# Adding batch 0's band mask on TensorE instead of multiplying it on VectorE, with k's rows in natural order

## The chip, the cores and the metric

The kernel runs on one core of one Trainium2 chip. Times are device microseconds (us) of a whole execution. The median of three executions of the kernel before was 313.24 us (312.52 to 313.91); with the fourth that ran beside the changed kernel, 313.38, it is 313.31. Executions of one kernel agree to some tenths of a per cent. "PE" is TensorE, "PEld" its weight load, "DVE" VectorE, "ACT" ScalarE, "POOL" GpSimd, "SP" SyncE. A profile has a span 1.7 to 2.0 us shorter than the time of the execution that it was taken from.

## The reference

```python
# q_l, k_l, v_l: (8, 8, 512, 64); q_g, k_g, v_g: (8, 8, 32, 64); all f32
mask = np.abs(pos[:, None] - pos[None, :]) <= 32      # band, for local x local
s_ll = np.where(mask, scale * q_l @ k_l.T, -1e9)
s_lg = scale * q_l @ k_g.T
out_l = softmax([s_lg, s_ll]) @ [v_g; v_l]            # local queries
out_g = softmax(scale * q_g @ [k_g; k_l].T) @ [v_g; v_l]
x = concat([out_g, out_l]) -> (8 * 544, 512)          # heads side by side
h = x @ w_in                                          # 512 -> 2048
g = h * sigmoid(1.702 * h)
out = g @ w_out                                       # 2048 -> 512, f32
```

Attention over a band of 32 positions to either side and 32 global positions is followed by a two-layer MLP. The MLP's matmuls are most of the work.

## The kernel before

The eight heads of a batch are two units ("quads") of four heads; `a` is unit 0 and `c` is unit 1 of batch 0. For a quad, `Tk` and `Tq` transpose k and q on DVE, `S(rnd)` makes half of the scores on PE (key blocks 0 and 1, or 2 and 3, each against a window of queries), `X` takes the exp on ACT, `M` multiplies by the 0/1 band mask on DVE, `K` and `XK` do the global keys, `U` and `ekU` multiply by v. Row position is split as 16 r + t for queries and, before, in 4 r + t for keys.

```python
kf = k_l.rearrange("b (u j) (c r t) d -> b j r u c (t d)", j=4, c=4, t=4)
vf = v_l.rearrange("b h (c r t) d -> b t r h c d", c=4, t=4)
...
load(0, kq=False)
q32 = ld.tile([128, 16 * D], F32, name="q32", bufs=1)
nc.scalar.dma_start(out=q32, in_=qf[0][:, 0])        # q of unit 0, f32, ScalarE's queue
load_g32(0, "qk")                                     # globals, SyncE's queue
load_g32(0, "v", eng=nc.scalar)
for j in range(4):
    load_k(0, 0, j)                                   # k of unit 0, to bf16, POOL's queue
...
keep(62, psP.tile([128, 512], F32, name="w", tag="p"), 128)   # warm-up matmuls
...
def Tk(self, cs=(0, 1, 2, 3)):
    ...
    nc.vector.transpose(self.kT[:, cs], rk[:, cs])    # keys stay in the order (t r)

def S(self, rnd, split=False, warm=0):
    ...
    for c in (2 * rnd, 2 * rnd + 1):
        for e in range(2):
            for j in range(4):
                nc.tensor.matmul(ps[j][:, off : off + n * nr],
                                 lhsT=self.k[p, 128 * c : 128 * c + 128, e],
                                 rhs=self.q[p, t0 : t0 + n, r0 : r0 + nr, e],
                                 start=(e == 0), stop=(e == 1), skip_group_check=True)

def M(self, rnd, lo=0, hi=LW):
    e = self.E[rnd][:, :, at + lo : at + hi]
    nc.vector.tensor_mul(e, e, mask[:, rnd : rnd + 1, lo:hi].to_broadcast(...))
...
# batch 0, in program order (cut)
make_mb(); cast_q(0); cast_q(1); make_mask()          # masks built ahead of all else
... a.S(0); a.X(0); a.S(1, split=True, warm=4); a.X(1)
... a.M(0); c.Tq(); c.gg(); c.S(0); c.X(0); a.M(1)
load_g32(1, "qkv", hold=True)
... c.S(1); c.X(1, halves=True) ... c.M(0) ... c.M(1, 0, 192); c.M(1, 192)
... # then the first four h steps of the MLP, fc = 0 to 3, and fc = 4 to 15
```

The softmax here doesn't subtract the row's maximum and nothing guards it: scores larger than these inputs give would overflow.

## Time and profile before

| | before |
|---|---|
| median time | 313.24 us |
| span of the profile | 310.7 us |
| PE busy | 97% |
| first S of unit 0 / of unit 1 | 7.90 / 11.81 us |
| first h matmul of the MLP | 20.19 us |
| first matmul of the second MLP layer | 34.41 us |
| first S of batch 2 | 66.01 us |

The stages in this table are start times from the span's start, read from the timeline of PE. Two lines of the page of the kernel before will be needed later; the prediction shows the rest. The first is the granted PE clock in 40 slices of the span, the second a group of instructions (shapes, count, busy us and mean ns, idle time before).

```profile
PEclk9999999999999999999999999999999999999999
...
L260 DVE STREAM_TRANSPOSE kT<-rk 128x512 f32<-128x512 f32 (+1 forms) x17 | 11.4, 671 | 0.0
```

### The profile page before, as it was taken

Reading aid. Unit: us, or ns where it says so; the run is one execution under the profiler, and the core shown is the slowest. Engines: PE = TensorE matmul, PEld = TensorE weight load, DVE = VectorE, ACT = ScalarE, POOL = GpSimd, SP = SyncE. Lnnn points to the kernel's source line nnn. Section 1 sums busy time; section 2 is a strip of 40 time slices with the busy share of each in tenths; the row PEclk is TensorE's granted clock in tenths of the full one; section 3 lists DMA queues with packets and bytes.
Section 4 is the critical chain, followed back from the end, with each engine's and each line's share of the span. In section 5 each row is a group of like instructions: output and inputs, shape, how many; then the busy total and the mean of one; then the engine's idle time right before and its main releaser. Section 6 shows DMA issues by size and latency. Waiting matters only on the chain.

```text
span 310.7 us, 7885 instructions
## 1 busy us (share of the span) xinstructions
PE 302.8 (97%) x3257; PEld 148.6 (48%) x3257; DVE 210.4 (68%) x463; ACT 167.3 (54%) x254; POOL 80.0 (26%) x131
## 2 busy tenths in 40 slices
PE   7899999999999999999999999999999999999995
PEld 6444444444554454444454455444454454446653
DVE  7887946869867866776957866776767855574320
ACT  4817465476536744565446735565556652563321
POOL 8822579677146000900045001200000000000000
PEclk9999999999999999999999999999999999999999
DMA  8999999999969212970279113901120012201123
GB/s 154 149 189 207 206 161 193 165 147 129 151 77 168 45 36 61 139 108 12 60 77 169 30 36 71 102 0 31 41 49 23 0 38 55 48 0 29 41 61 76
DMA packets 60099, 27.44 MB, mean 88 GB/s; under 512 B 43296, under 2 KB 51744, under 8 KB 60064
## 3 DMA queue, kind: packets, MB, share of 16 engines
q0 software_dynamic: 51536, 17.11, 50.7%
q1 hardware_dynamic: 7904, 9.12, 11.9%
q10 hardware_dynamic: 624, 0.72, 0.8%
q8 instruction: 25, 0.41, 0.5%
q14 instruction: 10, 0.08, 0.1%
HBM read 35.13 MB, written 8.91 MB: 142 GB/s over the span
## 4 chain that ended last, share of the span: by engine, by line
PE 91%; DVE 3%; ACT 2%; DMA 1%; POOL 1%; issue 0%; ACTq 0%; DVEq 0%; POOLq 0%
PE op L482 37%; PE hp L457 36%; PE s L291 6%; PE ov L389 5%; PE ov L367 3%; DMA rk<-in_k_l_dram 1%; PE s L457 1%; ACT e L322 1%; PE kb L310 1%; DVE e L329 1%; PE op L494 1%; PE s L310 1%; DVE gT L465 1%; PE s L406 1%; POOL rk L84 1%; PE ov L162 1%
## 5 line engine op out<-in xcount | busy, mean ns | idle before, releaser
L482 PE MATMUL op<-w_out_sb,gT 128*128 128x512 bf16 x528 | 121.9, 380 | 0.1
L465 DVE SCALAR_TENSOR_TENSOR gT<-th,hp 128x512 bf16<-128x512 f32 (+1 forms) x140 | 91.1, 655 | 43.0 <-ACT th L464 42.4
L457 PE MATMUL hp<-xL,w_in_sb 128*128 128x512 bf16 x496 | 108.6, 379 | 0.3 <-DVE xL L421 0.3
L464 ACT ACTIVATE th<-hp 128x512 f32<-128x512 f32 (+1 forms) x140 | 79.9, 573 | 43.7 <-PE hp L457 41.2
L457 PEld LDWEIGHTS <-w_in_sb 128*128 128x128 bf16 x576 | 56.1, 98 | 65.1 <-issue 1.2
L482 PEld LDWEIGHTS <-gT 128*128 128x128 bf16 x528 | 49.3, 98 | 56.2 <-issue 3.3
L322 ACT ACTIVATE e<-s 128x1712 bf16<-128x1712 f32 (+2 forms) x32 | 49.6, 1552 | 15.8 <-PE s L406 8.9
L496 ACT ACTIVATE ob<-op 128x512 f32<-128x512 f32 (+2 forms) x35 | 20.5, 585 | 61.6 <-PE op L482 59.1
L97 POOL DMA_DIRECT2D v<-in_v_l_dram x36 | 27.0, 757 | 96.2 <-PE s L406 88.9
L84 POOL DMA_DIRECT2D rk<-in_k_l_dram x64 | 34.9, 557 | 12.3 <-DMA w_in_sb<-in_moe_w_in_dram 4.7
L329 DVE TENSOR_TENSOR e<-e,mask 128x1408 bf16<-128x1408 bf16 (+2 forms) x33 | 28.0, 851 | 6.9 <-ACT e L322 6.7
L412 DVE STREAM_TRANSPOSE sT<-ov 128x512 f32<-128x512 f32 x16 | 11.4, 714 | 31.3 <-PE ov L389 31.3
L291 PE MATMUL s<-q,kT 32*128 32x200 bf16 (+1 forms) x512 | 21.3, 284 | 1.5 <-DVE kT L260 0.9
L421 DVE TENSOR_TENSOR xL<-ov,rs 128x512 bf16<-128x512 f32 x32 | 20.7, 685 | 2.2 <-PE ov L389 0.9
L291 PEld LDWEIGHTS <-kT 32*128 32x128 bf16 x512 | 10.9, 95 | 14.7 <-issue 9.1
L357 ACT ACTIVATE ek<-kb 128x512 bf16<-128x512 f32 x16 | 9.6, 600 | 8.4 <-PE kb L310 8.4
L389 PE MATMUL ov<-e,v 128*32 128x192 bf16 (+1 forms) x512 | 13.1, 240 | 0.0
L416 DVE STREAM_TRANSPOSE rs<-rT 128x512 f32<-128x512 f32 x16 | 11.4, 711 | 0.6
L260 DVE STREAM_TRANSPOSE kT<-rk 128x512 f32<-128x512 f32 (+1 forms) x17 | 11.4, 671 | 0.0
L263 DVE STREAM_TRANSPOSE q<-rq 128x512 f32<-128x512 f32 (+1 forms) x17 | 10.9, 647 | 0.0
L389 PEld LDWEIGHTS <-v 128*32 128x32 bf16 x512 | 9.8, 97 | 2.0 <-issue 2.0
L310 PE MATMUL kb<-q,kgT 32*32 32x512 bf16 x128 | 10.0, 385 | 0.5 <-ACT e L319 0.5
(71 smaller groups left out, 155.5 us busy)
## 6 DMA issues: line engine op xcount, KB each, us to landing
out_dram<-ob SPq DMA_DIRECT2D x132, 64.0 KB, 1.7
rk<-in_k_l_dram POOLq DMA_DIRECT2D x64, 64.0 KB, 4.0
v<-in_v_l_dram POOLq DMA_DIRECT2D x28, 128.0 KB, 4.5
rq<-in_q_l_dram POOLq DMA_DIRECT2D x6, 512.0 KB, 6.7
w_in_sb<-in_moe_w_in_dram POOLq DMA_DIRECT2D x4, 512.0 KB, 11.7
w_out_sb<-in_moe_w_out_dram POOLq DMA_DIRECT2D x4, 512.0 KB, 13.4
rq<-in_q_l_dram POOLq DMA_DIRECT2D x3, 256.0 KB, 7.9
q<-in_q_l_dram ACTq DMA_DIRECT2D x1, 512.0 KB, 3.9
```

The costliest lines, as they stand in the source:

```text
L84: nc.gpsimd.dma_start(out=loaded[b][0][32 * j : 32 * j + 32, u], in_=kf[b, j][:, u])
L97: nc.gpsimd.dma_start(out=vtiles[b % 2][p, s, :, :, :D], in_=vf[b, t][:, hs])
L291: nc.tensor.matmul(ps[j][:, off : off + n * nr], lhsT=self.k[p, 128 * c : 128 * c + 128, e], rhs=self.q[p, t0 : t0 + n, r0 : r0 + nr, e], ...
L322: nc.scalar.activation(e[:, :, lo:hi], self.ps[:, :, lo:hi], AF.Exp, scale=scale)
L329: nc.vector.tensor_mul(e, e, mask[:, rnd : rnd + 1, lo:hi].to_broadcast([128, 4, hi - lo]))
L389: nc.tensor.matmul(ov[32 * j : 32 * j + 32, :].rearrange("p (t r) -> p t r", t=16)[:, :, r0 : r0 + nr], lhsT=lv, rhs=self.E[c // 2][:, j, ...
L421: nc.vector.tensor_mul(self.x[:, 2 * self.u + h, :], self.st[1 + h], self.st["rs"])
L457: nc.tensor.matmul(hp[:, : width(i)], lhsT=w_in_c[:, fc // 8, kc, fc % 8 // 2, :, fc % 2], rhs=(xL[i] if i < B else xG)[:, kc, :], start=( ...
L464: nc.scalar.activation(th[:, :n], hp[:, :n], AF.Tanh, scale=0.851)
L465: nc.vector.scalar_tensor_tensor(gTs[i][:, fc, :n], in0=th[:, :n], scalar=1.0, in1=hp[:, :n], op0=ALU.add, op1=ALU.mult)
L482: nc.tensor.matmul(op, lhsT=gTs[i][:, fc, tci * 128 : tci * 128 + 128], rhs=w_out_sb[:, fc, :], start=(first and fc == 4 * f4), stop=(fc = ...
L496: nc.scalar.activation(ob[:, lo:hi], op[:, lo:hi], AF.Copy, scale=0.5)
```

## The change

The intent: take four mask multiplies and the building of the mask off the ladder of engines that leads to the first h matmul. In batch 0 the band is added to the scores as a large negative bias, by an identity matmul that opens each PSUM accumulation (`B`). For that the keys have to lie in natural order, so that one band serves all blocks; k is therefore written in that order by its transpose (and v is read in that order). The 0/1 mask that later batches need is built by ACT among batch 0's h steps. In passing, half of k of unit 0 is loaded as f32 from SyncE, v of unit 0 comes ahead of that of unit 1, and the first half of w_in comes in narrower pieces.

```diff
-    vf = v_l.rearrange("b h (c r t) d -> b t r h c d", c=4, t=4)
+    vf = v_l.rearrange("b h (c t r) d -> b t r h c d", c=4, t=4)
...
+    k32 = ld.tile([128, 2, 4 * D], F32, name="k32", bufs=1)
+    load_g32(0, "q")
     for j in range(4):
-        load_k(0, 0, j)
+        nc.sync.dma_start(out=k32[32 * j : 32 * j + 32], in_=kf[0, j][:, 0, 0:2])
+    load_g32(0, "kv")
...
-    keep(62, psP.tile([128, 512], F32, name="w", tag="p"), 128)
+    keep(44, psP.tile([128, 512], F32, name="w", tag="p"), 128)
...
+    nc.vector.tensor_sub(ident, step[:, 65:193], step[:, 64:192])
+    nc.vector.tensor_sub(band, step[:, 65:257], step[:, 0:192])
+    nc.vector.tensor_scalar(bias, band, -1.0, 240000.0, op0=ALU.add, op1=ALU.mult)
+
+    def window(t, c):
+        y0 = 0 if c else 32
+        return t[:, y0 : y0 + 16 * WIN[c][1]].rearrange("p (r t) -> p t r", t=16)
...
-            nc.vector.transpose(self.kT[:, cs], rk[:, cs])
+            nc.vector.transpose(self.kT[:, cs].rearrange("p (c r t) -> p c t r", r=32, t=4), rk[:, cs])
...
+        def B(self, rnd, split=False, cs=(0, 1)):
+            ...
+                for j in range(4):
+                    nc.tensor.matmul(ps[j][:, w : w + 16 * WIN[c][1]], lhsT=ident, rhs=window(bias, c),
+                                     start=(c == 2 * rnd), stop=False, skip_group_check=True)
...
-    a.S(0)
+    a.B(0)
+    a.B(1, split=True)
+    a.S(0, added=True)
...                      # likewise c.B(0), and c.B(1) in two halves; a.M, c.M of batch 0 gone
-    load_g32(1, "qkv", hold=True)    # moved to after a.R()
...
     for fc in range(4, FC):
         h_step(0, fc)
+        if fc in (5, 6, 8, 9):
+            make_mask((5, 6, 8, 9).index(fc))
```

`window(bias, c)` reads the bias with its inner index 16 elements apart, that is every 32 bytes in bf16. The output of the transpose of k goes to every fourth f32, that is every 16 bytes.

More of the change, by code (lines that the diff above doesn't have):

```diff
@@ L135 @@
     q32 = ld.tile([128, 16 * D], F32, name="q32", bufs=1)
-    nc.scalar.dma_start(out=q32, in_=qf[0][:, 0])
-    load_g32(0, "qk")
-    load_g32(0, "v", eng=nc.scalar)
-    for j in range(4):
-        load_k(0, 0, j)
-    mk = consts.tile([32, 208], BF16)
-    nc.vector.memset(mk, 1.0)
-    for sg, base in ((1, 2 * W + 3), (-1, -3)):
-        nc.gpsimd.affine_select(
-            out=mk, in_=mk, pattern=[[-sg, 208]], compare_op=ALU.is_ge,
-            fill=0.0, base=base, channel_multiplier=4 * sg,
-        )
+    for hf in range(2):
+        f = slice(8 * D * hf, 8 * D * hf + 8 * D)
+        nc.scalar.dma_start(out=q32[:, f], in_=qf[0][:, 0, f])
+    k32 = ld.tile([128, 2, 4 * D], F32, name="k32", bufs=1)
+    load_g32(0, "q")
+    for j in range(4):
+        nc.sync.dma_start(out=k32[32 * j : 32 * j + 32], in_=kf[0, j][:, 0, 0:2])
+    load_g32(0, "kv")
+    step = consts.tile([128, 257], BF16)
+    nc.vector.memset(step, 1.0)
+    nc.gpsimd.affine_select(
+        out=step, in_=step, pattern=[[1, 257]], compare_op=ALU.is_ge,
+        fill=0.0, base=-65, channel_multiplier=-1,
+    )
+    for j in range(4):
+        nc.gpsimd.dma_start(out=loaded[0][0][32 * j : 32 * j + 32, 0, 2:4], in_=kf[0, j][:, 0, 2:4])
     load(0, (1,))
@@ L173, with make_mask @@
     WIN = ((0, 10), (6, 12), (14, 12), (22, 10))
-    mb = consts.tile([128, 16, 12], BF16)
     mask = consts.tile([128, 2, LW], BF16)
-    def make_mb():
-        for k in range(4):
-            nc.vector.tensor_copy(mb[32 * k : 32 * k + 32],
-                                  mk[:, 3 - k : 195 - k].rearrange("p (r t) -> p t r", t=16))
-    def make_mask():
-        at = 0
-        for c, (r0, nr) in enumerate(WIN):
-            lo = r0 - 8 * c + 2
-            nc.scalar.activation(
-                mask[:, c // 2, at : at + 16 * nr].rearrange("p (t r) -> p t r", t=16),
-                mb[:, :, lo : lo + nr], AF.Copy)
-            at = (at + 16 * nr) % LW
+    ident = consts.tile([128, 128], BF16)
+    band = consts.tile([128, 192], BF16)
+    bias = consts.tile([128, 192], BF16)
+    nc.vector.tensor_sub(ident, step[:, 65:193], step[:, 64:192])
[4 more added lines that the diff above has]
+        return t[:, y0 : y0 + 16 * WIN[c][1]].rearrange("p (r t) -> p t r", t=16)
+    def make_mask(c):
+        nr = WIN[c][1]
+        at = (0, 160, 0, 192)[c]
+        nc.scalar.activation(mask[:, c // 2, at : at + 16 * nr].rearrange("p (t r) -> p t r", t=16),
+                             window(band, c), AF.Copy)
     ones32 = consts.tile([128, 32], BF16)
@@ L214, in load_rest @@
     def load_rest():
-        load_v(0)
-        for part in range(2):
-            cs = slice(part * (d_ff // 2), (part + 1) * (d_ff // 2))
+        vp = v_l[0].rearrange("(u h) (c p) d -> u p h c d", u=2, p=128)
+        for u in range(2):
+            for p in (slice(0, 64), slice(64, 128)):
+                nc.gpsimd.dma_start(out=vtiles[0][p, u, :, :, :D], in_=vp[u, p])
+        half = d_ff // 2
+        for part, lo, hi in ((0, 0, 512), (0, 512, half), (1, 0, half)):
             for u in range(2):
-                nc.gpsimd.dma_start(out=w_in_sb[:, part, 2 * u : 2 * u + 2, :], in_=w_in_r[u][:, :, cs])
+                nc.gpsimd.dma_start(out=w_in_sb[:, part, 2 * u : 2 * u + 2, lo:hi],
+                                    in_=w_in_r[u][:, :, part * half + lo : part * half + hi])
         for g4 in range(4):
@@ L249, in __init__ @@
             self.E = [None, None]
+            self.bk = {}
             self.st = {}
@@ L275, in ext, with S @@
                     qgT[:, self.Q, : n * nr].rearrange("p (t r) -> p t r", t=n))
-        def S(self, rnd, split=False, warm=0):
-            if split:
-                ps = [pbank("s") for _ in range(4)]
-                keep(warm, ps[0])
-            else:
-                pt = self.spt(rnd)
-                ps = [pt[:, j, :] for j in range(4)]
-            off = 0
-            for c in (2 * rnd, 2 * rnd + 1):
+        def B(self, rnd, split=False, cs=(0, 1)):
+            if cs[0] == 0:
+                self.bk[rnd] = [pbank("s") for _ in range(4)] if split else self.spt(rnd)
+            ps = self.bk[rnd] if split else [self.bk[rnd][:, j, :] for j in range(4)]
+            for c in [2 * rnd + i for i in cs]:
+                w = (40, 200, 36, 228)[c]
+                for j in range(4):
+                    nc.tensor.matmul(ps[j][:, w : w + 16 * WIN[c][1]], lhsT=ident, rhs=window(bias, c),
+                                     start=(c == 2 * rnd), stop=False, skip_group_check=True)
+        def S(self, rnd, split=False, added=False, cs=(0, 1)):
+            if not added and cs[0] == 0:
+                self.bk[rnd] = self.spt(rnd)
+            ps = self.bk[rnd] if split else [self.bk[rnd][:, j, :] for j in range(4)]
+            for c in [2 * rnd + i for i in cs]:
+                off = (0, 200, 0, 228)[c]
                 r0, nr = WIN[c]
@@ L294, in S @@
                             rhs=self.q[p, t0 : t0 + n, r0 : r0 + nr, e],
-                            start=(e == 0), stop=(e == 1), skip_group_check=True,
+                            start=(e == 0 and not added), stop=(e == 1), skip_group_check=True,
                         )
-                off += n * nr
+            if cs[0] == 0:
+                self.E[rnd] = att.tile([128, 4, RW + 32], BF16, name="e%d" % rnd)
             if split:
                 self.gk(ps[2][:, RW : RW + 32], self.qg)
-            self.ps = ps if split else pt
-            self.E[rnd] = att.tile([128, 4, RW + 32], BF16, name="e%d" % rnd)
+            self.ps = self.bk[rnd]
         def gk(self, out_, rhs, e=None):
@@ L312, in gk, with X @@
                                      start=(ee == 0), stop=(ee == 1), skip_group_check=True)
-        def X(self, rnd, halves=False):
+        def X(self, rnd, part=None):
             e = self.E[rnd]
@@ L320, in X @@
                 return
-            for lo, hi in ((0, 228), (228, RW)) if halves else ((0, RW),):
+            for lo, hi in ((0, RW),) if part is None else ((228 * part, 228 + 200 * part),):
                 nc.scalar.activation(e[:, :, lo:hi], self.ps[:, :, lo:hi], AF.Exp, scale=scale)
-            if rnd == self.gr:
+            if rnd == self.gr and not part:
                 nc.scalar.activation(e[:, 2, RW:], self.ps[:, 2, RW : RW + 32], AF.Exp, scale=scale)
@@ L517, in cast_q @@
         nc.scalar.activation(rq[:, 0, f], q32[:, f], AF.Copy)
-    make_mb()
     cast_q(0)
     cast_q(1)
-    make_mask()
+    nc.scalar.activation(rk[:, 0, 0:2], k32, AF.Copy)
     cast_g32(0, "q")
@@ L533 @@
     load_rest()
-    a.S(0)
+    a.B(0)
+    a.B(1, split=True)
+    a.S(0, added=True)
     a.X(0)
-    a.S(1, split=True, warm=4)
+    a.S(1, split=True, added=True)
     a.X(1)
     c.ext()
+    c.Tk()
     cast_g32(0, "v")
-    c.Tk()
+    c.Tq()
+    c.B(0)
     a.K()
     a.XK()
-    a.M(0)
-    c.Tq()
+    c.S(0, added=True)
     c.gg()
-    c.S(0)
     c.X(0)
-    a.M(1)
-    load_g32(1, "qkv", hold=True)
     a.eg()
-    c.K(0)
+    c.K()
+    c.XK()
     a.ekU(0)
-    c.K(1)
-    c.XK()
     a.U(0)
     a.R()
+    load_g32(1, "qkv", hold=True)
     a.ekU(1, 3)
-    c.S(1)
-    c.X(1, halves=True)
-    a.ekU(2, 4)
+    c.B(1, cs=(0,))
+    c.S(1, added=True, cs=(0,))
+    c.X(1, part=0)
     a.U(1)
+    a.XL(0)
+    c.B(1, cs=(1,))
+    c.S(1, added=True, cs=(1,))
+    c.X(1, part=1)
+    a.ekU(2)
     a.U(2)
+    a.XL(1)
     a.Gm()
-    c.M(0)
-    a.XL(0)
-    c.M(1, 0, 192)
-    c.M(1, 192)
-    a.XL(1)
     gTs[0] = moe.tile([128, FC, TB], BF16, name="gT")
```

## The prediction

> **What bounds the kernel now.** First the page: PE is busy 97% of 310.7 us at full clock, and the chain of work that ended last is PE for 91% of the span.
>
> ```profile
> PE 302.8 (97%) x3257; PEld 148.6 (48%) x3257; DVE 210.4 (68%) x463; ACT 167.3 (54%) x254; POOL 80.0 (26%) x131
> PE   7899999999999999999999999999999999999995
> DMA  8999999999969212970279113901120012201123
> PE 91%; DVE 3%; ACT 2%; DMA 1%; POOL 1%; issue 0%; ACTq 0%; DVEq 0%; POOLq 0%
> ```
>
> Only the first three of the 40 slices (7.8 us each) leave PE short of full, and there DMA is full too. The diff touches little beyond them, so second the chain of waits in order of time (start, length, what):
>
> ```profile
> 3.08 3.98 DMA rk<-in_k_l_dram
> 7.13 0.38 DVE q L263
> 7.51 0.34 DVE kT L260
> 7.90 0.69 PE s L291 x16
> 8.61 1.61 ACT e L322
> 10.24 0.89 DVE e L329
> 11.14 0.63 DVE q L263
> 11.81 0.67 PE s L291 x16
> ...
> 20.26 3.56 PE s L457 x16
> 23.82 0.28 PE og L406 x20
> 24.10 10.47 PE hp L457 x48
> 34.57 4.32 PE op L482 x20
> ```
>
> Batch 0 attention is a ladder of engines until 20.2 us; then the MLP runs with hardly a pause: 48 matmuls in 10.47 us are 0.218 us each, near the 0.216 us spacing of unbroken ones. So the time is about 20.2 us of start plus 290 us of PE work, and the change can win only what it takes off the start and what PE keeps of it afterwards.
>
> Third the timeline, for what PE will meet when it is earlier. POOL may have eight transfers open, so an issue that waits for the transfer eight before it shows when that landed:
>
> ```profile
> 19.11 0.54 POOL L84 DMA_DIRECT2D rk<-in_k_l_dram  x1 [2.39 <-DMA w_in_sb<-in_moe_w_in_dram]
> 21.98 0.55 POOL L84 DMA_DIRECT2D rk<-in_k_l_dram  x1 [2.33 <-DMA w_in_sb<-in_moe_w_in_dram]
> 24.83 0.55 POOL L88 DMA_DIRECT2D rq<-in_q_l_dram  x1 [2.30 <-DMA w_in_sb<-in_moe_w_in_dram]
> 27.70 0.71 POOL L221 DMA_DIRECT2D w_out_sb<-in_moe_w_out_dram  x1 [2.33 <-DMA w_in_sb<-in_moe_w_in_dram]
> ```
>
> These are the four pieces of w_in; the landing records themselves say 18.83, 21.69, 24.54 and 27.42, one each 2.86 us. The DMA view of the window from 8 to 28 us has the engines at nine tenths or more in all but one slice. Who needs the pieces: the h steps for fc = 4 onward start at 24.03 with four matmuls each, so fc = 8 starts at 24.03 + 16 x 0.216 = 27.48, and its third matmul, the first to read the fourth piece, at 27.91. That piece landed 0.49 us earlier. **This 0.49 us is the slack that I hold to be decisive.**
>
> **What the Trainium skill says.** "TensorE: Matmul & The Clock Gate", section "Back-to-back issue gap": N/1.2 ns when cold and N/2.4 + 2.5 ns when warm. The trace agrees: the 128-column warm-up matmuls start 107 ns apart until 5.4 us and 55 ns apart after. "DMA: Bandwidth & Descriptors", section "Issuing engines are not separate DMA queues": another issuing engine saves only its issue time, the same 16 engines move the data. The trace fits: with SyncE, ScalarE and POOL all issuing, one full set of engines is seen. "Perfetto Trace Analysis", section "DMA Optimizations", says that splitting lets parts start sooner if the engines are generally idle; here they are full, so splitting w_in reorders arrival and adds no rate. "SBUF — State Buffer", section "Door 1", says an access that goes to a new 16-byte line each time pays a penalty: the new bias windows are read at a stride of 32 bytes, and the transposes of k are written at 16. Nothing in this trace shows what either costs on its engine.
>
> **The change, part by part.**
>
> 1. Start of S(0). Before, rqg's cast began at 5.90, behind four mask copies of 0.32 us that waited for POOL; S(0) came 2.0 us later, at 7.90. After, those copies are gone and that DVE sequence can start when the global q has landed (5.11 before, first on its queue in both): 5.1 + 2.0 = 7.1. The other feeders fit: 256 KB of k u0 as f32 on SyncE should land near 5.2, and ScalarE casts it after two q casts of 0.6 us, by about 6.1. PE: 44 warm-ups, 37 at 107 ns and 7 at 55, end near 5.8; then 16 identity matmuls of 160 or 192 columns at 69 and 82 ns, 1.2 us, end near 7.0. So S(0) at 7.1, **0.8 us earlier**.
>
> 2. Mask multiplies. Four of them in batch 0 leave DVE: 0.89 + 0.89 + 0.85 + 0.95 = 3.6 us. On the path were the first, which held c.Tq until 11.14, and part of the last, for which PE stood 0.3 us at 18.1. In their place PE gets 16 more identity matmuls, of which c.B(0) fits under the second softmax and the eight of c.B(1) lie on the path, 0.3 us each half.
>
> 3. c.S(0) was at 11.81. It needs q of unit 1, which landed at 10.58 behind the same bytes. Transposing costs 0.70: c.S(0) near 11.2, gain **0.6 us**; the other 0.2 is lost to the transfer.
>
> 4. c.X(0) then ends at 13.5 instead of 14.1, c.S(1) in two halves at 14.2 and 15.7 with the first exp between. v of unit 0 comes as the first two of four pieces, near 13, so a's U(1) fits beside it rather than waiting for all of v (15.70). From the end of the last S of c, about 15.8, follow U(2), Gm and three ekU+U groups, 0.85 + 0.4 + 2.6 us, so the first h near 19.6: gain **about 0.6 us**, with 0.2 to 1.1 possible. The narrower w_in pieces (256 KB each for fc 0 to 7, near 17.3, 18.8, 20.2 and 21.7) serve that.
>
> 5. Then the slack. With a gain of 0.6, fc = 8 asks for the last w_in at 27.3; bytes ahead of it are the same, except 128 KB more written for k and 256 packets of k moved off the slow path: by the packets' own times (512 B at about 60 ns, 4096 B f32 at 159 ns, over 16 engines) that is at most 0.3 us to the good. Landing then 27.1 to 27.4, plus the usual 0.05 to 0.1. PE stands for 0 to 0.2 us. **Kept: about 0.5 us.**
>
> 6. After that, w_out pieces, k, q and v of batch 1 had over 1 us to spare (w_out's last landed at 40.50 and is read near 41.8), so the 0.5 us should reach the end. Mask building moves into h steps of batch 0: four ScalarE copies that take about 0.25 us each in a row, where ScalarE had 0.27 us idle a step; casts at fc = 7 add 0.6 us, which four PSUM banks should absorb.
>
> Sum: 313.24 - 0.5 = 312.7 us.
>
> **The rivals.**
>
> Rival A, the strided reads. If each column at a 32-byte stride takes twice as long, the first 16 identity matmuls take 2.4 us and S(0) comes at 8.3, and each half of c.B(1) costs 0.3 more: no gain, or 313.6. For it: the skill's line; DVE's copies of the same stride took 0.32 us for 192 elements where a contiguous 128 took 0.18. Against it: the warm-ups were cut by 18 matmuls, about 1.0 us, which looks like room for 16 at 75 ns.
>
> Rival B, a wait in place of the one removed: the h phase fully bound by w_in. If the stream lands as before or later, all beyond 0.4 us is given back as a wait at fc = 8; if w_in's finer packets are slower, the result is 313.2 to 313.7. For it: 0.49 us of slack. Against: per byte, 512 B and 2048 B packets of cast loads flow alike (1.40 us per 256 KB against 2.86 per 512 KB).
>
> Rival C, ScalarE: the globals of batch 1 are now loaded after R, some 2 us later than the 12.95 of before; they took 9 to 13 us to land, the last at 27.97, and ScalarE casts them in order at fc = 7. If they land past 29, tanh stops, the four banks fill and PE loses up to 1 us: 313.5. For it: those slow landings. Against: their packets alternate with w_in's, and smaller ones let them through sooner.
>
> Rival D, more gain: with v's rows read in natural order, the v load (5.1 us between q and w_in, the least efficient stretch) shortens by 0.5 to 1 us, so w_in lands earlier and PE keeps its whole 0.6 to 1.1 us: 312.2. Against: packets stay 256 B read, 128 B written.
>
> **Range and chances.** The middle is 312.7. The parts spread from -1.1 (D) to +0.5 (A, B or C), and before alone varied from 312.52 to 313.91, so 8 in 10 for 311.4 to 313.9. Two per cent is 6.3 us, more than half of the whole stretch that the ladder could shorten, and nothing recurring per batch is added but a stride in one 0.70 us transpose of DVE, which has slack: faster 0.01, same 0.98, slower 0.01.
>
> **What would show it right or wrong.** S(0) near 7.1 and identity matmuls 70 to 82 ns apart confirm step 1; 140 ns or more is Rival A. c.S(0) waiting for the transpose of q, near 11.2, confirms step 3. First h matmuls near 19.6 confirm step 4. A PE wait at the third matmul of fc = 8, ended by w_in's last landing near 27.3, confirms step 5; a wait of tanh for the batch 1 global casts is Rival C; w_in's last piece landing before 26.8 is D. The prediction fails most likely in step 5, if the DMA stream is not the same length as before, or in step 4, where the order of PE, ScalarE and DVE was laid out by hand.

## The result, and the profile after

The changed kernel took 321.52 us (320.65 to 322.88, four executions) against 313.31 us (312.52 to 313.91) of the kernel before beside it. The ratio is 1.0268, with a 95% interval of 1.0219 to 1.0316: slower. All ratios here are the mean time of one kernel's fast executions over that of the other's of the same rounds, so they are not quite the ratio of the medians quoted.

The page of the changed kernel: busy totals, two of the rows in 40 slices (8.0 us each), and two groups.

```profile
PE 312.4 (98%) x3263; PEld 151.1 (47%) x3263; DVE 211.9 (66%) x457; ACT 168.3 (53%) x255; POOL 80.9 (25%) x132
...
PE   8899999999999999999999999999999999999995
...
PEclk9669999999999999999999999999999999999999
...
L271 DVE STREAM_TRANSPOSE kT<-rk 128x512 f32<-128x512 f32 (+1 forms) x17 | 17.9, 1054 | 1.1 <-ACT rk L540 1.0
...
L296 PE MATMUL s<-bias,ident 128*128 128x160 bf16 (+1 forms) x32 | 10.8, 494 | 1.4 <-ACT e L341 1.4
```

PE is busier than before, in time and in share: 312.4 us instead of 302.8 with only six matmuls more. The 32 identity matmuls are 10.8 us of that, 494 ns as the mean length of one. The clock row has two slices at six tenths where the kernel before has nine in every slice. And the transpose of k takes 1054 ns where it took 671. None of these three sizes was in the prediction's sum.

The chain of waits of the changed kernel in order of time (start, length, what):

```profile
6.41 5.04 PE s L296 x16
11.45 0.86 PE s L310 x16
12.31 0.02 issue
12.33 1.61 ACT e L341
13.94 0.04 issue
13.98 2.69 PE s L296 x8
16.66 0.97 PE kb L329 x8
17.64 0.83 PE s L310 x16
...
21.68 1.47 PE s L296 x4
23.15 0.40 PE s L310 x8
...
24.55 1.31 PE s L296 x4
...
29.34 3.56 PE s L476 x16
```

The identity matmuls (L296) stand on the chain with 5.04 + 2.69 + 1.47 + 1.31 = 10.5 us. The first 16 alone take 5 us, where the prediction had 1.2. Their starts in the trace are 287 to 293 ns apart for 160 columns and 342 to 346 ns for 192: 1.8 ns a column, before 7.34 us, when the clock is still at half, and after it, when it is at full. So it isn't the array's clock that sets this pace.

The view by stretches of the changed kernel (us; busy us and count on PE, PEld, DVE, ACT and POOL; then the granted clock, DMA share, GB/s):

```profile
6.20:11.40 5.20, 5.20 (x22) 1.85 (x23) 4.01 (x13) 0.63 (x1) 5.20 (x8) 0.94 1.48 151
...
14.00:17.60 3.60, 3.60 (x20) 1.01 (x23) 0.23 (x1) 1.63 (x4) 1.79 (x3) 0.50 1.19 185
...
21.60:29.30 7.70, 7.09 (x145) 3.08 (x142) 3.16 (x9) 1.77 (x2) 1.80 (x3) 1.00 1.13 209
```

The clock is at half from 10.75 to 20.99 us, although PE shows as busy without a gap in the first stretch: 5.20 of 5.20 us. It had been full for only 3.41 us. Everything on PE in this time is slower too: 16 matmuls of S take 0.83 to 0.86 us, where they took 0.67 to 0.69.

### The profile page after: what moved, and what is told of

Its sections match the earlier page's. It is cut to its first block, busy times and chain, and to the rows that moved or that the text cites. A ratio compares the mean times of both kernels' runs of the same rounds, so it can differ in the third digit from the quotient of the medians.

```text
span 320.3 us, 7903 instructions
## 1 busy us (share of the span) xinstructions
PE 312.4 (98%) x3263; PEld 151.1 (47%) x3263; DVE 211.9 (66%) x457; ACT 168.3 (53%) x255; POOL 80.9 (25%) x132
## 3 DMA queue, kind: packets, MB, share of 16 engines
q0 software_dynamic: 51824, 16.98, 48.9%
## 4 chain that ended last, share of the span: by engine, by line
PE 93%; DVE 3%; ACT 2%; issue 0%; ACTq 0%; DVEq 0%
PE op L501 36%; PE hp L476 34%; PE s L310 6%; PE ov L408 5%; PE s L296 3%; PE ov L386 3%; PE w L166 2%; ACT e L341 1%; PE s L476 1%; PE kb L329 1%; DVE gT L484 1%; PE op L513 1%; PE s L329 1%; PE s L425 1%; ACT th L483 0%
## 5 line engine op out<-in xcount | busy, mean ns | idle before, releaser
L97 POOL DMA_DIRECT2D v<-in_v_l_dram x32 | 23.8, 755 | 104.4 <-PE s L425 97.2
L84 POOL DMA_DIRECT2D rk<-in_k_l_dram x60 | 32.5, 549 | 12.2 <-DMA v<-in_v_l_dram 4.8
L348 DVE TENSOR_TENSOR e<-e,mask 128x1408 bf16<-128x1408 bf16 x28 | 24.4, 873 | 5.6 <-ACT e L341 5.6
L271 DVE STREAM_TRANSPOSE kT<-rk 128x512 f32<-128x512 f32 (+1 forms) x17 | 17.9, 1054 | 1.1 <-ACT rk L540 1.0
L296 PE MATMUL s<-bias,ident 128*128 128x160 bf16 (+1 forms) x32 | 10.8, 494 | 1.4 <-ACT e L341 1.4
L274 DVE STREAM_TRANSPOSE q<-rq 128x512 f32<-128x512 f32 (+1 forms) x17 | 11.2, 658 | 0.7 <-ACT rq L536 0.4
```

What stands on the lines that cost most here:

```text
L84: nc.gpsimd.dma_start(out=loaded[b][0][32 * j : 32 * j + 32, u], in_=kf[b, j][:, u])
L97: nc.gpsimd.dma_start(out=vtiles[b % 2][p, s, :, :, :D], in_=vf[b, t][:, hs])
```

## The experiments

Nine kernels were run (no run is called e5). Ratios are against the kernel before on the same chip. The stages of the profiled runs, in us from the span's start:

| | S(0) | c.S(0) | first h | second layer | S of batch 2 | end |
|---|---|---|---|---|---|---|
| before | 7.90 | 11.81 | 20.19 | 34.41 | 66.01 | 310.67 |
| after | 11.38 | 17.57 | 29.27 | 43.48 | 75.50 | 320.27 |
| e1_contig_bias | 8.17 | 11.99 | 20.45 | 34.66 | 67.17 | 311.92 |
| e2_no_identity | 7.66 | 12.99 | 21.93 | 36.51 | 68.67 | 313.15 |
| e4_contig_x4 | 10.32 | 15.77 | 26.04 | 40.25 | 72.25 | 317.16 |
| e6_contig_transpose | 7.61 | 12.08 | 20.53 | 34.74 | 66.34 | 310.89 |
| e7_late_casts | 7.97 | 12.61 | 21.06 | 35.27 | 67.33 | 312.00 |
| e8_permuted_identity | 7.61 | 12.18 | 19.91 | 35.72 | 67.33 | 311.88 |
| e9_v_four_pieces | 7.70 | 12.35 | 20.07 | 34.58 | 66.43 | 310.98 |
| e10_k_by_pool | 8.15 | 12.98 | 20.88 | 35.40 | 67.15 | 312.20 |

Two theories stood at first. Theory 1: the stride of the bias windows is the whole loss, by the reading itself and by the clock that falls because of it. Theory 2: other parts of the change cost as well (its loads, the strided transposes, the order of work), or PE's new place on the ladder does whatever it reads.

### e1_contig_bias: the same change with contiguous bias windows

```diff
-    nc.vector.tensor_scalar(bias, band, -1.0, 240000.0, op0=ALU.add, op1=ALU.mult)
+    for c in (0, 1, 3):
+        nc.vector.tensor_scalar(bias[BW[c]].rearrange("p (t r) -> p t r", t=16), window(band, c),
+                                -1.0, 240000.0, op0=ALU.add, op1=ALU.mult)
...
-  lhsT=ident, rhs=window(bias, c),
+  lhsT=ident, rhs=bias[BW[c]],
```

> The changed kernel with one thing altered: the bias windows are written out once by VectorE as contiguous rows, so the 32 identity matmuls read their 160 or 192 columns one after another instead of at a stride of 32 bytes. Theory 1 (the strided read costs 1.79 ns a column, and the drop of the clock follows from it): identity matmuls start 69 to 82 ns apart instead of 285 to 345, the clock stays full, S(0) starts near 7.5 us instead of 11.4, the first h matmul near 20 us instead of 29.3, and the time falls to 312 to 313.5 us. Rival (other parts of the change cost as well: the f32 load of k, the order of v, the narrower w_in, the strided transposes): the time stays above 315 us.

Measured: 314.78 us (313.63 to 315.4), ratio 1.0047 (1.0011 to 1.0082), clock 0.999 to 1.0 in every execution. PE's timeline of this run:

```profile
6.20 2.04 PE L300 MATMUL s<-bias,ident 128*128 128x160 bf16 x16
8.17 1.16 PE L314 MATMUL s<-q,kT 32*128 32x200 bf16 x32
```

The 16 identity matmuls take 2.0 us in place of 5.2; the first nine still ran at half clock, 133 or 160 ns apart, the rest 69 or 83. Some 6.7 of the 8.2 us are thus the stride of one operand and what follows from it, and the clock no longer falls. But the kernel is still 0.5% behind the one before, which is 1.5 us by the ratio and 2.0 by the medians, so theory 2 holds for that remainder.

### e2_no_identity: masks back on DVE, all else as changed

```diff
-    a.B(0)
-    a.B(1, split=True)
-    a.S(0, added=True)
+    a.S(0)
...
+    a.M(0)      # likewise a.M(1), c.M(0), c.M(1); masks made by ACT ahead of S; 62 warm-ups
```

> The changed kernel without the identity matmuls: batch 0 is masked by multiplies on VectorE as in the kernel before, all other parts of the change kept (natural key order, f32 half of k, v by unit, narrower w_in, 62 warm-up matmuls again). Theory 1 expects 312 to 314 us, near the kernel before, and a clock that stays full from its first rise. The rival (other parts cost) expects 315 us or more.

Measured: 315.09 us (314.31 to 315.63), ratio 1.0059 (1.0026 to 1.0091). With no identity matmul at all there is still a loss like that of e1, so some other part of the change costs. How much of it is the same as in e1 this run can't tell: its masks are back on DVE, and while PE waited for q of unit 1 its clock fell to half from 12.76 to 16.17 us. On DVE's timeline of this run the transpose of unit 1's q waits for its load, which landed at 12.20 us (before: 10.58):

```profile
12.22 0.71 DVE L274 STREAM_TRANSPOSE q<-rq 128x512 f32<-128x512 f32 x1 [1.17 <-DMA rq<-in_q_l_dram]
```

### e3_stride_probe: what a strided moving operand costs by itself

The kernel before, with 56 matmuls of 512 columns after its warm-ups, which read the same 512 bf16 in a different order:

```diff
+    for T, n in ((1, 8), (2, 8), (4, 8), (8, 8), (16, 16), (1, 8)):
+        for _ in range(n):
+            nc.tensor.matmul(pw, lhsT=warm[:, 0:128], rhs=warm.rearrange("p (r t) -> p t r", t=T),
+                             start=True, stop=True)
```

> The kernel before with a probe behind its warm-up: 8 matmuls of 128 x 128 by 512 columns for each inner stride of the moving operand of 1, 2, 4 and 8 bf16 elements, 16 of stride 16 (the stride of the bias windows), and 8 of stride 1 again. Theory 1: stride 1 to 4 start 216 ns apart at full clock, stride 16 start about 920 ns apart (1.79 ns a column), stride 8 lies between or at either; the 14 us of stride 16 make the clock fall to half although the page calls PE busy, and the last 8 of stride 1 then start 427 ns apart at first. If instead the slow identity matmuls had another cause (the accumulation into PSUM, a port shared with VectorE), stride 16 starts 216 ns apart here. The whole time should rise by 20 to 25 us.

Measured once: 344.7 us, 32 more than before, so the guess of 20 to 25 was too low. The distances from start to start in its trace, in ns:

```
inner stride   1    2    4    8   16        1 (again, at half clock)
bytes          2    4    8   16   32        2
ns           216  226  452  900  918      427
```

A stride of 4 bytes costs 5%, one of 8 bytes doubles the time and one of 16 bytes quadruples it; 32 bytes adds little more. This is where the guess failed: it had inner stride 4 at 216 ns, and left stride 8 open. The view by stretches of this run (the last three numbers are clock, DMA share, GB/s) shows the clock:

```profile
7.00:17.00 10.00, 10.00 (x38) 3.24 (x36) 2.91 (x14) 0.00 (x0) 8.36 (x13) 1.00 1.58 154
17.00:41.00 24.00, 24.00 (x47) 4.21 (x46) 0.00 (x0) 0.08 (x1) 9.55 (x17) 0.50 1.20 201
```

The clock fell to half at 16.98 us, 2.4 us into the matmuls of stride 8, and came back at 40.87 us, 4.4 us after the contiguous ones had begun again (36.45). PE is shown busy for all of the 24 us. VectorE worked for only 0.08 us of them, and no matmul of the probe adds to an earlier one, so neither of the two other causes that the expectation names is needed. The matmuls of stride 8 stayed 900 ns apart on both sides of the fall. So strided reading is slow at either clock, and it takes the clock down with it, which then hits the contiguous work behind it: 427 ns in place of 216.

### e4_contig_x4: each identity matmul four times, contiguous

This puts the time of the slow reading back without the stride, to tell its direct cost from that of the clock.

```diff
-    nc.tensor.matmul(..., rhs=bias[BW[c]], start=(c == 2 * rnd), ...)
+    for rep in range(4):
+        nc.tensor.matmul(..., rhs=bias[BW[c]], start=(c == 2 * rnd and rep == 0), ...)
```

> As the first run, but each identity matmul is issued four times over (the mask becomes four times as large, which exp does not feel), so that it takes 277 to 330 ns of array time, about what the strided one takes, with the array really at work. It parts the cost of the time itself from the cost of the clock. Theory 1: the clock stays full, and what the half clock cost in the changed kernel (about 2 us in the matmuls between 11 and 21 us) is saved: 319 to 320 us. Rival (the clock drop is the main loss): 316 us or less. Rival (the clock does not matter): 321.5 us, as the changed kernel.

Measured: 319.23 us (318.65 to 319.5), ratio 1.0191 (1.0155 to 1.0228), clock 0.997 to 1.0. PE's timeline, and below it the clock (1.00) in the stretch:

```profile
5.37 5.02 PE L301 MATMUL s<-bias,ident 128*128 128x160 bf16 x64
10.32 1.16 PE L315 MATMUL s<-q,kT 32*128 32x200 bf16 x32
```
```profile
6.00:10.30 4.30, 4.30 (x58) 4.18 (x55) 2.50 (x12) 1.26 (x2) 3.27 (x6) 1.00 1.05 141
```

64 contiguous matmuls occupy PE for 5.02 us, as 16 strided ones do, yet the clock stays full and what follows runs at its full speed. From e1 to e4 the time grew by 319.23 - 314.78 = 4.4 us: that is the slow reading itself. From e4 to the changed kernel it grew by 321.52 - 319.23 = 2.3 us: that is the clock. The two kernels ran in different calls, and the changed kernel's four times spread over 2.2 us, so the second figure is the rougher one. Two things bear it out. In the table, the way from S(0) to the first h is 17.89 us in the changed kernel and 15.72 in e4, 2.2 us less; the other 1.1 us between these two profiles lies before S(0), where the clock first rose at 7.34 and at 4.44 us, and that first rise varied from run to run with the same warm-ups. And the changed kernel's own executions are the longer the lower their mean clock: 320.65 and 320.80 us at 0.989, 322.24 at 0.984, 322.88 at 0.978. It is also an upper one, since four contiguous matmuls at 69 and 82 ns are 276 and 330 ns, some 12 ns short of a strided one, or up to 0.4 us for all 32.

### e6_contig_transpose: e1 with the transpose of k contiguous

The keys then stand in the wrong order for the bias, so the result is wrong.

```diff
-  nc.vector.transpose(self.kT[:, cs].rearrange("p (c r t) -> p c t r", r=32, t=4), rk[:, cs])
+  nc.vector.transpose(self.kT[:, cs], rk[:, cs])
```

> The run e1_contig_bias with one thing more undone: the transposes of k write their 512 columns in a row again instead of at a stride of 16 bytes. The keys are then in an order that the mask does not match, so the result is wrong on purpose. Theory 2 (what is left of the loss, 1.5 us, comes from VectorE's strided transposes, 1.09 to 1.18 us each instead of 0.70, which push back the h steps of batch 1): the transposes take 0.70 us again, the first S of batch 2 comes 8.7 us after the first h of batch 1 as in the kernel before (not 9.6), and the time falls by about 1 us from the 314.8 us of e1_contig_bias. Rival (VectorE has slack, the loss lies in the casts and mask copies on ScalarE): no change from e1_contig_bias.

Measured: 313.32 us (312.86 to 313.83), ratio 1.0007 (0.9989 to 1.0025): the kernel before's time. It passed the comparison with the reference all the same. So the comparison doesn't resolve this error, likely because the attention averages many small values of v, and its passing is no proof of the mask's order in the other kernels. The transpose in batch 1's h steps and the S that waits behind it, first in e1 and then here:

```profile
61.55 1.18 DVE L275 STREAM_TRANSPOSE kT<-rk 128x512 f32<-128x512 f32 x1
...
67.17 0.67 PE L314 MATMUL s<-q,kT 32*128 32x200 bf16 x16 [0.85 <-DVE q L288]
```
```profile
61.44 0.70 DVE L275 STREAM_TRANSPOSE kT<-rk 128x512 f32<-128x512 f32 x1
...
66.34 0.67 PE L314 MATMUL s<-q,kT 32*128 32x200 bf16 x16
```

In e1 DVE is so dense there that the transpose's extra 0.48 us, with the work that it pushes on, reaches PE: S of batch 2 waits 0.85 us. Counted from the first h matmul of batch 1 with a bank of its own (57.53 and 57.42 us), S of batch 2 comes 9.64 us later in e1 and 8.93 here, which is what the kernel before has. By the medians the strided transposes cost 314.78 - 313.32 = 1.5 us; by the two ratios (each against the kernel before on its own chip), 0.4% or 1.3 us. Of that 0.7 us is seen at this one place in e1, the rest is spread. In the changed kernel itself the same distance is 75.50 - 66.14 = 9.36 us, and in e7 9.39, so there this place costs only 0.4 us more than before: 1.5 us is an upper figure for the changed kernel.

### e7_late_casts: e1 with the casts of batch 1's globals three steps later

The globals of batch 1 are issued about 2.6 us later than before. In e1 ACT waited for the last of them:

```profile
29.45 0.31 ACT L130 ACTIVATE rvg<-g32v 128x128 bf16<-128x128 f32 x1 [0.45 <-DMA g32v<-in_v_g_dram]
```

```diff
-        if fc == 7:
+        if fc == 10:
             cast_g32(1, "qkv")
```

> The run e1_contig_bias with the ScalarE casts of batch 1's globals moved from fc = 7 to fc = 10 and their transposes from 10 to 11, so that tanh does not stand behind a transfer that landed at 29.37 us. Rival theory 3 (the wait of ScalarE at fc = 7, 0.45 us, and what it pushes back cost the time): falls by 0.4 to 0.8 us from e1_contig_bias. Theory 2: no change beyond 0.2 us.

Measured: 314.27 us (312.86 to 314.97), ratio 1.0034 (0.9998 to 1.007). The wait of ACT is gone from the timeline, but the interval covers both e1's value and no loss at all. Rival C exists as a wait of 0.45 us. From the first h matmul to the second layer both kernels need 14.21 us, so PE lost nothing by it there; and e6, which has the time of before, has the same wait (0.51 us) and the same 14.21. A longer one may cost: in e2, where ACT waits 1.07 us, that way takes 14.58 us.

### e8_permuted_identity: a version meant to win

If the rows of the identity are permuted instead of the keys, k can be transposed contiguously in the order of before and the result is right. The 0/1 mask is made by the same matmul and an exp. Bias contiguous, casts late, 30 warm-ups, v again in the rows of before, in eight pieces.

```diff
-    nc.vector.tensor_sub(ident, step[:, 65:193], step[:, 64:192])
+    nc.vector.tensor_sub(ident.rearrange("p (t r) -> p t r", t=4),
+                         step[:, 65:193].rearrange("p (r t) -> p t r", t=4),
+                         step[:, 64:192].rearrange("p (r t) -> p t r", t=4))
```

> A version meant to win: contiguous bias windows; the key order of the kernel before, so that transposes are contiguous, with the mask brought into that order by a permuted identity in the matmul; masks of later batches made by two such matmuls and two ScalarE passes; the casts as in e7_late_casts; 30 warm-ups; the second S of unit 1 in one piece. Theories 1 and 2 expect S(0) near 7.5 us, first h matmul at 19.6 to 20 us, and 312.2 to 313 us, at or a little under the kernel before. If the start of the h phase does not come before 20.2 us, the ladder is bound by the landing of q of unit 1 (10.6 to 11.2 us) and no mask scheme can win here.

Measured: 314.36 us (313.76 to 314.96), ratio 1.004 (1.0021 to 1.0059): not faster. The first h matmul came at 19.91 us, the only version to beat the 20.19 of before by more than 0.2, and then PE waited:

```profile
20.82 1.47 PE L483 MATMUL s<-xL,w_in_sb 128*128 128x512 bf16 x6 [0.53 <-DMA w_in_sb<-in_moe_w_in_dram]
...
29.08 0.61 PE L483 MATMUL hp<-xL,w_in_sb 128*128 128x512 bf16 x2 [0.42 <-DMA w_in_sb<-in_moe_w_in_dram]
```

Eight small pieces of v had filled the eight open transfers, so the issues of w_in stood behind them, and its last piece landed at 29.04 us where before has 27.42. It is Rival B of the prediction in the flesh: the second wait is at the third matmul of fc = 8, just where the prediction looked for it.

### e9_v_four_pieces: e8 with v in four pieces

```diff
-        load_v(0, (0,))
-        load_v(0, (1,))
+        load_v(0)
```

> As e8_permuted_identity, but v of batch 0 in the four pieces of the kernel before instead of eight, so that the issues of w_in no longer wait behind it for one of the eight open transfers. Theory 1 (e8's loss was w_in: last piece at 29.04, PE waiting 0.53 us at 20.8): w_in's last piece lands before 27.5, no wait at the first h steps, first op at 34.3 or earlier, and the time is 0.9 to 1.5 us below e8's: 312.7 to 313.4, the same as before or 0.3 better. Theory 2 (something else in e8 holds the h stage, as ScalarE's late casts or the clock): first op stays later than 35 and the time stays at 314 or more.

Measured: 313.14 us (312.9 to 313.77, six executions) beside 312.89 of before, ratio 1.0007 (0.9984 to 1.003). The last w_in landed at 26.27 us and PE no longer waits for it:

```profile
20.07 3.63 PE L482 MATMUL s<-xL,w_in_sb 128*128 128x512 bf16 x16
```

Theory 1 held on the time, 1.2 us below e8; the second layer's start, 34.58, is 0.28 later than the limit that I had named, because the mask's own matmuls now stand among the h steps (14.51 us from the first h, not 14.21). So the best version of the idea equals the kernel before and does not beat it. Its ladder still has c.S(0) 0.5 us late.

### e10_k_by_pool: e9 with k of unit 0 loaded as before

Every variant has c.S(0) later than the 11.81 us of before, and q of unit 1 lands at 10.84 to 12.20 us instead of 10.58. This run asks whether the f32 half of k is to blame. One thing moves with it: POOL issues these four loads ahead of the select from which identity and bias are made, so VectorE starts on the bias at 4.66 us, not 2.94.

```diff
-    k32 = ld.tile([128, 2, 4 * D], F32, name="k32", bufs=1)
-    for j in range(4):
-        nc.sync.dma_start(out=k32[32 * j : 32 * j + 32], in_=kf[0, j][:, 0, 0:2])
+    for j in range(4):
+        load_k(0, 0, j)
```

> As e9_v_four_pieces, and k of unit 0 wholly in bf16 from POOL's queue as in the kernel before: no f32 half on SyncE, no cast of it on ScalarE. Theory 1 (the f32 half, 128 KB more to move ahead of q of unit 1, is what makes that q land 0.3 to 0.7 us later than the 10.58 of before): q lands at 10.4 to 10.7 and c.S(0) starts at 11.4 to 11.8; S(0) starts at 7.3 to 7.9, by k's landing. Theory 2 (the later landing has another cause, as when POOL can issue, or the globals' place on the queues): q still lands at 11.0 or later and c.S(0) at 12 or later. Time 312.5 to 314.5 either way.

Measured: 313.48 us (313.23 to 313.92), ratio 1.0013 (0.998 to 1.0045). Theory 1 falls by its own sign: q landed at 11.38 us. DVE's timeline shows the wait for it, and PE's the start of c.S(0) at 12.98, without idle time before it:

```profile
11.41 0.71 DVE L277 STREAM_TRANSPOSE q<-rq 128x512 f32<-128x512 f32 x1 [1.34 <-DMA rq<-in_q_l_dram]
```
```profile
12.98 0.90 PE L313 MATMUL s<-q,kT 32*128 32x200 bf16 x16
```

So q was ready at 12.12 us, and the rest of the delay is PE's own: c.B(0) and `K` ahead of c.S(0) ran at half clock, 1.33 and 1.04 us in place of the 0.77 and 0.63 of e1. S(0) too was late, 8.15 us, as it stood behind the later VectorE.

What makes that load late in all versions stays open. The issue of it came at 6.20 us here and at 6.71 in the kernel before, so POOL isn't late; the place of the globals on the queues, q of unit 0 in two pieces and the narrower w_in are still different, and no run separates them.

The last three kernels have a loss in common: with the strided bias gone, the clock fell to half in them too, from 10.47 to 13.88 us in e8, 9.86 to 13.27 in e9 and 8.06 to 14.89 in e10. In e9 q was ready at 12.29 us and PE free for c.S(0) at 12.35, so both held it. Why the clock fell isn't shown. These three have 30 warm-ups and PE stands idle twice before c.B(0), for 0.78 and 0.98 us in e9; but e6, with 44 warm-ups and waits of 1.03 and 0.78 us before c.S(0), kept its clock. So "equals the kernel before" holds for e9 as built; whether it would win with a full clock and an earlier q was not run.

## Why the prediction was wrong

It said 312.7 us and the kernel took 321.52, outside its range of 311.4 to 313.9. It called "faster", "same" and "slower by over 2%" with 0.01, 0.98 and 0.01, and the last came true.

**Step 1 failed, and with it the sum.** Its words were "then 16 identity matmuls of 160 or 192 columns at 69 and 82 ns, 1.2 us". The runs showed 288 and 345 ns, 5.2 us in all. Contiguous operands do run at 69 and 82 ns (e4, e6), so the length of each was mis-sized by the stride alone. Another feeder of S(0) was also off: SyncE's half of k landed at 6.2 to 6.4 us in all runs that have it but e4, not 5.2, and in the changed kernel its cast ended at 6.93, not 6.1, so that even without identity matmuls S(0) came at 7.66 (e2), not 7.1.

**Rival A had the right mechanism and the wrong size.** It read the stride as a factor of two, and so at most 313.6 us. The factor is 4.2. It was put aside with "the warm-ups were cut by 18 matmuls, about 1.0 us, which looks like room for 16 at 75 ns": an argument from what the author of the change seems to have expected, not from a measurement. The honest reading was the prediction's own earlier sentence, that nothing in the trace showed the cost of such a read on PE; a factor that is not known then belongs into the range. At a factor of four the same sum gives 16 x (0.069 + 0.082) / 2 x 3 = 3.6 us more for the first 16 alone.

**The clock was missing altogether.** No step or rival thought of it, since PE was to be busy. It accounts for about 2 us (e4 against the changed kernel).

**Step 2** was right for what it took away (no mask multiply of batch 0 is left on DVE) and wrong for what it put there: c.B(0) was not hidden but 2.69 us on the chain, and the halves of c.B(1) took 1.47 and 1.31 us in place of 0.3. In e1 the halves of c.B(1) are back at 69 and 82 ns a matmul.

**Step 3** fails even without the stride. "c.S(0) near 11.2, gain 0.6 us" assumed q of unit 1 to land at 10.58 again; it landed at 10.84 in the changed kernel, 11.29 in e6 and 11.56 in e9, and c.S(0) came at 12.08 and 12.35 in the last two, later than before.

**Step 4**, first h at 19.6, wasn't reached by any version: 29.27 in the changed kernel, 20.53 in e6, 19.91 in e8.

**Step 5**, the wait at fc = 8, was never seen in the changed kernel, because PE came 9 us later than it was to, while w_in's last piece landed at 26.46 us. Rival B did show itself in e8, as soon as PE was early and w_in late; in e9, w_in landed before 26.8, as Rival D would have it, though v is read there in the rows of before, so D's reason isn't shown; and no gain came of it, since the ladder had little to give (first h 0.12 us earlier).

**Step 6**, with the range built on it, said that nothing recurring costs "but a stride in one 0.70 us transpose of DVE, which has slack". The transpose took 1.09 to 1.19 us, and DVE did not have the slack in batch 1's h steps: 1.3 to 1.5 us from e1 to e6. The four mask copies took 0.49 to 0.56 us and not 0.25; no loss was traced to them.

The account of the 8.2 us: slow reading of the bias 4.4, the clock that falls with it 2.3 at most, strided transposes 1.5 at most, and nothing left over, since e6 with all three undone has the time of before. The three are differences of medians along one row of kernels, so that they sum up is no check of each by itself. The 0.5 us that the change was to gain is not in e6 or e9 either: in e6 PE stands 0.78 us for the late q of unit 1, in e9 that q and the half clock hold c.S(0) alike.

## What to carry to other kernels

Look at the innermost stride of every operand that a new matmul reads, and of every transpose's output, before counting columns: lay the data out contiguously once, by the engine that makes it, as e1 does with three writes of the bias in place of one, or permute the other operand, as e9 does. A PE that the page calls fully busy may take four times as long for the same matmul, as in e3; compare the distance of its matmuls with that of the warm-ups, and look at the clock row. And a ladder that waits for one late load, as e2, e6 and e7 do for q of unit 1, gives nothing back for work removed beside it.

## What the Trainium skill lacked or had wrong

- "SBUF — State Buffer", section "Door 1", gives the free stride as up to 4 f32 or 8 bf16, by lines of 16 bytes. For reads of PE's moving operand the probe shows otherwise: 216 ns for 512 bf16 at stride 1, 226 at stride 2, but 452 already at stride 4 (8 bytes), 900 at 8 and 918 at 16. For DVE's writes, the transpose of 128x512 f32 into every fourth f32 took 1.09 to 1.19 us in place of 0.70.
- "TensorE: Matmul & The Clock Gate", section "Back-to-back issue gap", gives the gap by the number of columns and the clock. It fits contiguous operands (69 and 82 ns for 160 and 192 columns at full clock) and lacks the stride of the moving operand: 1.8 ns a column at 32 bytes, the same at full and at half clock. Its part on the clock gate ties the clock to how busy PE has been; with strided reads the clock fell to half at 10.75 us of the changed kernel and at 16.98 us of the probe, while the profile showed PE busy without a gap.
